# A shorter exponential on VectorE: one of three tensor products taken out of each group, by reading the score's bits as fp16

## The chip, the cores and the metric

One core of one Trainium2 chip. The metric is device time in microseconds (us), the median of several runs. All runs quoted here are fast ones; one run of the kernel before, at 1364.4 us, was slow and is left out everywhere.

## The reference

A transformer block with pre-normalisation: softmax attention with 32 heads of 16, then a GELU-gated feed-forward part.

```
B, S, D, H = 1, 2048, 512, 32           # Dh = 16, F = 1792
scores = einsum("bhqd,bhkd->bhqk", q, k) * Dh ** -0.5
p = softmax(scores, axis=-1)
o = einsum("bhqk,bhkd->bhqd", p, v)
h  = x + o.reshape(B, S, D) @ wo
h2 = h + (gelu(ln(h) @ w_gate) * (ln(h) @ w_up)) @ w_down
```

## The kernel before

The scores are 2048 tiles of 128x512 in PSUM. Most are exponentiated by ScalarE, two or three tiles an instruction (`exps`). Some are given to VectorE, which has no exponential: it converts the scaled score to a 16-bit integer whose upper bits are the power of two and whose lower ten bits are the fraction (`dconv`), and makes the exponential from those bits with a chain of 16-bit operations over a *group* of up to four tiles (`dchain`). The result has two terms: E, the bare power of two, and T, E times an odd cubic of the mantissa. TensorE multiplies both with V and lets PSUM add them.

```
def dconv(G, j, b):                     # one tile, PSUM to SBUF
    Op("dve", 0.7, tensor_scalar(out=dX[...], in0=pbank[:, b, :],
       scalar1=1024.0 * CENTER, scalar2=0.0, op0=add, op1=max))
# ... (cut)
def dchain(G):                          # one group of n tiles
    t1, t2 = 0.16 + 0.133 * n, 0.16 + 0.267 * n
    yield Wait(lambda: G["conv"] == n)
    Op("dve", t1, E = (X >> 3) & 0x1f80)              # power of two, as bf16 bits
    Op("dve", t1, X = (X & 0x3ff) | 0x3c00)           # mantissa M, as fp16 bits
    Op("dve", t2, W = M * M)
    Op("dve", t1, W = W * EK + EB)
    Op("dve", t2, W = W * M)
    C["gw"] += 1
    Op("dve", t2, T = W * E)                          # written over X
    G["done"] = 1
```

The order of all instructions is not written by hand. It is planned while the kernel is built: every `Op` states an assumed duration (the number behind the engine's name), and a list scheduler places the operations one after another in that assumed time. On the chip each engine then works through its list in that order (checked for VectorE: its 600 conversions and chain instructions come exactly as planned). A tile goes to VectorE when the plan sees VectorE free, a PSUM bank free, and the group before it far enough. Three constants of the plan are `LAT` (assumed delay between dependent operations), `SLACK` (a further delay for some), and `LOOK` (how much later an operation of an older stream may start and still be preferred).

```
lim = st + LOOK                         # st: earliest possible start on this engine
for r, s in cands:                      # by priority, then by age
    if r <= lim: ...                    # this one is taken
LAT = 0.12; SLACK = 0.3; LOOK = 0.12
```

The GELU of the feed-forward part runs between the attention work: VectorE copies the gate from PSUM to SBUF, GpSimd makes three operations on it, ScalarE a tanh, VectorE the rest. A guard at the end checks that all softmax sums lie in a range; if not, a second, slower path does everything again.

Of the kernel before, what the change touches and what calls it, by code (L numbers as in the profile page):

```python
# [163 lines left out]
BF16 = mybir.dt.bfloat16  # L164
ACT = mybir.ActivationFunctionType
ALU = mybir.AluOpType
# [886 lines left out]
F16, U16 = mybir.dt.float16, mybir.dt.uint16  # L1053
GS = 4
NX = 3
# [4 lines left out]
DGAP = 6.0  # L1060
DBUSY = 2.0
LN2 = 0.6931471805599453
CENTER = 40
EC, EB, EK = 0.45805388, 1.01669147, 0.16656247
VSCALE = 2.0 ** (127 - CENTER)


def bass_sequential_preLN__mha_block__geglu_ffn__prompt_kernel(nc, A_x, A_wqkv, A_wo, B_x, B_w_gate, B_w_up, B_w_down, out):
# [37 lines left out]
def fast_path(nc, P, base0, ARENA, pbank, flag, A_x, A_wqkv, A_wo, B_x, B_w_gate, B_w_up, B_w_down, out):  # L1106
# [3 lines left out]
    def at(name, shape, dt, off=None):  # L1110
        nb = DTS[dt]
        for d_ in shape[1:]:
            nb *= d_
        if off is None:
            off = cur[0]
            cur[0] = (off + nb + 31) // 32 * 32
        assert off + nb <= ARENA, ("SBUF arena overflow", name, off, nb, ARENA)
        return nc.alloc_sbuf_tensor_at(name, shape, dt, offset=base0 + off)
# [5 lines left out]
    PT = at("PT", [128, NRING, 512], BF16)  # L1124
    offX = cur[0]
    dX = at("dX", [128, NX, GS, 512], U16)
# [3 lines left out]
    probe = at("probe", [128, 2], U16)  # L1130
# [35 lines left out]
    ident32 = at("ident32", [128, 128], FP32)  # L1166
# [13 lines left out]
    LINV = at("LINV", [128, NUNIT, 16], FP32)  # L1180
    LCHK = at("LCHK", [128, NUNIT * 16 + 1], FP32, offPT)
# [10 lines left out]
    NU = len(units)  # L1192
# [27 lines left out]
    def ACTF(o, i, func, **kw):  # L1220
        return lambda e: e.activation(out=o, in_=i, func=func, **kw)  # L1221
# [23 lines left out]
    def consts():  # L1245
        yield Op("pool", 0.5, lambda e: e.memset(ones_bf[:], 1.0), writes=["ones_bf"])
        yield Op("pool", 0.3, lambda e: e.affine_select(out=ident[:], in_=ones_bf[:, 0:128], pattern=[[1, 128]], compare_op=ALU.is_equal, fill=0.0,
                                                        base=0, channel_multiplier=-1), reads=["ones_bf"], writes=["ident"])
        yield Op("pool", 0.1, lambda e: e.memset(nhalf[:], -0.5), writes=["nhalf"])
        yield Op("pool", 0.2, lambda e: e.memset(LINV[:], 1.0), writes=[("LINV", u) for u in range(NU)])  # L1250
        yield Op("pool", 0.1, lambda e: e.memset(zero_bf[:], 0.0), writes=["zero_bf"])
        yield Op("pool", 0.3, lambda e: e.tensor_copy(out=ident32[:], in_=ident[:]), reads=["ident"], writes=["ident32"])
        yield Op("pool", 2.3, lambda e: e.memset(VA[:, :, :, 16:17], VSCALE), writes=["VA_ones"])

    def masks():
        for par in range(2):
            iv = ident32[:].rearrange("p (g x i) -> p g x i", g=4, x=2)[:, :, par, :]
            yield Op("dve", 0.2, lambda e, iv=iv, par=par: e.tensor_reduce(out=qmask[:, par:par + 1], in_=iv, axis=AX.XY, op=ALU.add), reads=["ident32"], writes=[("qm", par)])
            yield Op("dve", 0.1, lambda e, par=par: e.tensor_scalar(out=qmask[:, par:par + 1], in0=qmask[:, par:par + 1], scalar1=256.0 / LN2, scalar2=None, op0=ALU.mult),
                     reads=[("qm", par)], writes=[("qm", par)])  # L1260
        yield Op("dve", 0.5, lambda e: e.memset(pbank[:, PVB, :], 0.0), writes=[("pb", PVB)])
        yield Op("dve", 0.1, lambda e: e.tensor_scalar(out=probe[:, 0:1], in0=ident32[:, 0:1], scalar1=1e6, scalar2=0.0, op0=ALU.add, op1=ALU.max), reads=["ident32"], writes=["probe"])


    def ln1(c):
# [97 lines left out]
    def proj_v():  # L1363
        for t in range(NT):
# [3 lines left out]
            for hf in range(2):  # L1368
                yield Op("pe", 2 * TMM, cols=1024, fns=[MM(pbank[:, b, :], xnT[:, dc, 128 * t:128 * t + 128], wqkv_sb[:, dc, 2 * D:3 * D], dc == 0, dc == 3)
                                      for dc in (2 * hf, 2 * hf + 1)], reads=rd, writes=[("pb", b)])  # L1370
            op = Op("dve", 0.61, lambda e, b=b, t=t: e.tensor_scalar(out=VA[:, t, :, 0:16], in0=pbank[:, b, :].rearrange("p (h i) -> p h i", i=16), scalar1=VSCALE, scalar2=None, op0=ALU.mult),
                    reads=[("pb", b)], writes=[("V", t)])
# [23 lines left out]
    def qk():  # L1396
        nxt, an = 0, 0
        while nxt < len(TILES):
# [57 lines left out]
            for i, j, db in late:  # L1456
                sch.add(dconv(G, j, db), -2)
# [22 lines left out]
    def exps():  # L1480
        st = 0
        while "qkdone" not in C or st < len(STEPS):
            if st >= len(STEPS):
                yield Wait(lambda: st < len(STEPS))
            an, mine, b0 = STEPS[st]
            p0, n = an % NRING, len(mine)
            yield Op("act", 0.093 + 0.427 * n, ACTF(PT[:, p0:p0 + n, :], pbank[:, b0:b0 + n, :], ACT.Exp, scale=LN2 / 1024, bias=-LN2 * (127 - CENTER) - math.log(EC)),
                     reads=[("pb", b0 + k) for k in range(n)], writes=[("PT", p0 + k) for k in range(n)],
                     gate=lambda: C.get("qk", 0) >= st + 1 and C["acons"] >= an + n - NRING)
            st += 1  # L1490
            C["exp"] = st
            made.update(mine)
        C["expdone"] = 1
        sch.early = True
        for b0, n in SLOTS:
            for b in range(b0, b0 + n):
                sch.release(b)
# [26 lines left out]
                C["dbanks"].append(b)  # L1524

    def dconv(G, j, b):
        yield Op("dve", 0.7, lambda e: e.tensor_scalar(out=dX[:, G["k"] % NX, j, :], in0=pbank[:, b, :], scalar1=1024.0 * CENTER, scalar2=0.0, op0=ALU.add, op1=ALU.max),  # L1527
                 reads=[("pb", b)], writes=[("dX", G["k"] % NX, j)], gate=lambda: C["gpv"] >= G["k"] - NX + 1)
        sch.release(b)
        G["conv"] += 1  # L1530

    def dchain(G):

        d, x, n = G["k"] % NE, G["k"] % NX, len(G["t"])
        X, W, E = dX[:, x, 0:n, :], dW[:, 0:n, :], dE2[:, d, 0:n, :]
        M, T = X.bitcast(F16), X.bitcast(BF16)
        kX, kW, kE = [("dX", x, j) for j in range(n)], ["dW"], [("dE", d)]
        t1, t2 = 0.16 + 0.133 * n, 0.16 + 0.267 * n
        yield Wait(lambda: G["conv"] == n)
        yield Op("dve", t1, lambda e: e.tensor_scalar(out=E.bitcast(U16), in0=X, scalar1=3, scalar2=0x1f80, op0=ALU.logical_shift_right, op1=ALU.bitwise_and), reads=kX, writes=kE,  # L1540
                 gate=lambda: C["gpv"] >= G["k"] - NE + 1)
        yield Op("dve", t1, lambda e: e.tensor_scalar(out=X, in0=X, scalar1=0x3ff, scalar2=0x3c00, op0=ALU.bitwise_and, op1=ALU.bitwise_or), reads=kX, writes=kX)  # L1542
        yield Op("dve", t2, lambda e: e.tensor_tensor(out=W, in0=M, in1=M, op=ALU.mult), reads=kX, writes=kW)  # L1543
        yield Op("dve", t1, lambda e: e.tensor_scalar(out=W, in0=W, scalar1=EK, scalar2=EB, op0=ALU.mult, op1=ALU.add), reads=kW, writes=kW)
        yield Op("dve", t2, lambda e: e.tensor_tensor(out=W, in0=W, in1=M, op=ALU.mult), reads=kW + kX, writes=kW)  # L1545
        C["gw"] += 1
        yield Op("dve", t2, lambda e: e.tensor_tensor(out=T, in0=W, in1=E, op=ALU.mult), reads=kW + kE, writes=kX)  # L1547
        G["done"] = 1

    def pv():  # L1550
# [230 lines left out]
    def check():  # L1781
        yield Wait(lambda: C.get(("hnT", NC - 1), 0) == CHUNKS[-1] // 128)
        lf = LINV[:].rearrange("p u i -> p (u i)")
        n = NUNIT * 16
        yield Op("dve", 0.1, lambda e: e.tensor_scalar(out=LCHK[:, n:n + 1], in0=probe[:, 0:1], scalar1=65535.0, scalar2=None, op0=ALU.is_equal), reads=["probe"] + [("LINV", u) for u in range(NU)], writes=["probe", "LCHK"])
        yield Op("dve", 0.4, lambda e: e.tensor_scalar(out=LCHK[:, 0:n], in0=lf, scalar1=2.0 ** -22, scalar2=2.0 ** 16, op0=ALU.max, op1=ALU.min),
                 reads=[("LINV", u) for u in range(NU)], writes=["LCHK"])
        yield Op("dve", 0.6, lambda e: e.tensor_tensor(out=LCHK[:, 0:n], in0=LCHK[:, 0:n], in1=lf, op=ALU.is_equal), reads=["LCHK"], writes=["LCHK"])
        yield Op("dve", 0.6, lambda e: e.tensor_reduce(out=lmin[:, 0:1], in_=LCHK[:], axis=AX.X, op=ALU.min), reads=["LCHK", "probe"], writes=["lmin"])
        b = yield Acquire(reads=["lmin", "ones_bf"])  # L1790
        yield Op("pe", 0.1, lambda e: e.matmul(pbank[0:1, b, 0:1], lmin[:, 0:1], ones_bf[:, 0:1], start=True, stop=True), reads=["lmin", "ones_bf"], writes=[("pb", b)])
        yield Op("dve", 0.1, lambda e: e.tensor_copy(out=flag[0:1, 0:1], in_=pbank[0:1, b, 0:1]), reads=[("pb", b)], writes=["flag"])
        P.flag_count = P.eng["dve"].count
        sch.release(b)
# [88 lines left out]
```

## Time and profile before

| | before |
|---|---|
| time, median | 948.25 us (4 runs, 947.93 to 949.04) |
| score tiles on ScalarE / VectorE | 1832 / 216 (in 64 groups) |
| busy: ScalarE, VectorE, GpSimd | 874.4, 735.3, 220.5 us of 947.0 |
| last exponential ends at | 912 us; what follows ("the tail"): 35 us |

From the page of the kernel before, the busy times by engine and the engines' shares of the chain that ended last (the path of work and waits, followed back from the last instruction):

```profile
PE 833.2 (88%) x7100; PEld 276.3 (29%) x7224; DVE 735.3 (78%) x1138; ACT 874.4 (92%) x817; POOL 220.5 (23%) x268
...
ACT 33%; PE 32%; DVE 16%; issue 14%; POOL 5%; ACTq 0%; DVEq 0%; POOLq 0%
```

ScalarE (ACT) is the busiest, and the chain passes mostly through it and TensorE (PE); 16% of it lies on VectorE (DVE).

Groups of instructions of the kernel before (count, busy us, mean ns of one, idle time of the engine before them and its releaser). A mean mixes shapes where it says "forms":

```profile
L1221 ACT ACTIVATE PT<-pbank 128x1536 bf16<-128x1536 f32 (+1 forms) x733 | 841.0, 1306 | 24.8 <-PE pbank L1215 24.2
L1527 DVE TENSOR_SCALAR dX<-pbank 128x512 uint16<-128x512 f32 x216 | 146.8, 686 | 45.9 <-PE pbank L1215 45.0
L1719 POOL TENSOR_TENSOR w_sb<-w_sb,g_sb 128x512 f32<-128x512 f32 (+1 forms) x56 | 71.3, 1273 | 4.7
L1717 POOL TENSOR_TENSOR w_sb<-g_sb 128x512 f32<-128x512 f32 (+1 forms) x56 | 65.3, 1166 | 168.2 <-DVE g_sb L1715 168.2
L1547 DVE TENSOR_TENSOR dX<-dW,dE_56 128x2048 bf16<-128x2048 f16 (+3 forms) x64 | 73.2, 1144 | 1.0
L1545 DVE TENSOR_TENSOR dW<-dW,dX 128x2048 f16<-128x2048 f16 (+3 forms) x64 | 71.0, 1109 | 1.4
L1543 DVE TENSOR_TENSOR dW<-dX 128x2048 f16<-128x2048 f16 (+3 forms) x64 | 70.7, 1105 | 1.2
L1726 ACT ACTIVATE w_sb<-w_sb 128x512 f32<-128x512 f32 (+1 forms) x56 | 34.1, 609 | 12.4 <-POOL w_sb L1719 12.4
```

The first line is the exponentials, the second the conversions (one for each VectorE tile), the POOL (GpSimd) lines two of the GELU steps, the three products below them the ones of the chain (L1545 is the one that goes), the last line the tanh of GELU. ScalarE waited 24.8 us in all before exponentials and 12.4 us before tanh, the latter for GpSimd.

Busy time by engine in two 40 us stretches, one with attention only and one that also carries feed-forward work (columns: stretch, its length, then each engine's busy us and instructions, granted TensorE clock, DMA share and GB/s):

```profile
core 0: us, PE busy (x) PEld busy (x) DVE busy (x) ACT busy (x) POOL busy (x), PEclk, DMA share, GB/s
160.00:200.00 40.00, 34.49 (x272) 10.04 (x275) 36.56 (x48) 39.40 (x36) 0.00 (x0) 1.00 0.03 8
320.00:360.00 40.00, 35.91 (x242) 11.14 (x247) 29.22 (x41) 38.85 (x40) 21.58 (x19) 1.00 0.00 1
```

In the first, ScalarE and VectorE are both nearly full. In the second GpSimd works for half of the time.

### The profile page before, as it was taken

What the parts mean: (1) busy time and instruction counts of PE and PEld (TensorE: products, weight loads), DVE (VectorE), ACT (ScalarE), POOL (GpSimd) and SP (SyncE); (2) the same over time, 40 slices, a digit from 0 to 9 for tenths busy, and PEclk for the clock granted to TensorE, in tenths of its full rate; (3) what the DMA queues carried; (4) which work ended last, traced back from release to release, by engine and by line L of the source; (5) the groups of instructions that cost most, each with busy time, mean ns of one, the idle gap of its engine ahead of it and who ended that gap; (6) DMA issues with size and microseconds to landing.
All of it is one profiled execution on the core that took longest, in us unless ns stands there. A gap on an engine that the chain in (4) does not pass through costs nothing.

```text
span 947.0 us, 17699 instructions
## 1 busy us (share of the span) xinstructions
PE 833.2 (88%) x7100; PEld 276.3 (29%) x7224; DVE 735.3 (78%) x1138; ACT 874.4 (92%) x817; POOL 220.5 (23%) x268
## 2 busy tenths in 40 slices
PE   8999888888898889888888988998898788899887
PEld 3322222222232222222222222222233222333345
DVE  7558989998979768699979788889958687643753
ACT  5789999999999999999999998999999799999962
POOL 6400000000027570000014564000003354302440
PEclk9999999999999999999999999999999899999999
DMA  5000006000000000000000000000000000000000
GB/s 178 1 1 1 1 1 244 1 2 1 12 2 1 1 1 12 23 1 2 1 12 1 1 1 1 12 23 1 1 8 19 1 1 1 2 12 24 2 7 21
DMA packets 12331, 15.13 MB, mean 16 GB/s; under 512 B 1744, under 2 KB 11216, under 8 KB 12240
## 3 DMA queue, kind: packets, MB, share of 16 engines
q1 hardware_dynamic: 12240, 13.90, 4.5%
q8 instruction: 59, 0.97, 0.5%
q14 instruction: 32, 0.26, 0.1%
HBM read 11.80 MB, written 2.10 MB: 15 GB/s over the span
## 4 chain that ended last, share of the span: by engine, by line
ACT 33%; PE 32%; DVE 16%; issue 14%; POOL 5%; ACTq 0%; DVEq 0%; POOLq 0%
ACT PT L1221 32%; PE pbank L1215 15%; PE pbank L1214 11%; PE pbank L1801 4%; POOL w_sb L1717 2%; DVE dX L1527 2%; POOL w_sb L1719 2%; DVE dW L1543 2%; DVE dE_56 L1540 1%; DVE dX L1542 1%; DVE dX L1547 1%; DVE g_sb L1715 1%; ACT w_sb L1726 1%; POOL w_sb L1718 1%; DVE w_sb L1727 1%
## 5 line engine op out<-in xcount | busy, mean ns | idle before, releaser
L1221 ACT ACTIVATE PT<-pbank 128x1536 bf16<-128x1536 f32 (+1 forms) x733 | 841.0, 1306 | 24.8 <-PE pbank L1215 24.2
L1215 PE MATMUL pbank<-QT,KT 32*128 32x512 bf16 (+1 forms) x2560 | 287.1, 341 | 71.7 <-ACT PT L1221 57.5
L1215 PE MATMUL pbank<-PT,VA 128*17 128x512 bf16 (+1 forms) x2307 | 187.6, 340 | 3.2 <-issue 1.8
L1527 DVE TENSOR_SCALAR dX<-pbank 128x512 uint16<-128x512 f32 x216 | 146.8, 686 | 45.9 <-PE pbank L1215 45.0
L1215 PEld LDWEIGHTS pbank<-QT,KT 32*128 32x128 bf16 x2560 | 77.0, 91 | 319.3 <-ACT PT L1221 220.6
L1801 PE MATMUL pbank<-ones_bf,zero_bf 128*128 128x512 bf16 x388 | 135.2, 388 | 13.5 <-DVE OA L1613 11.0
L1678 POOL TENSOR_SCALAR rstd_102<-mv_101 128x1 f32<-128x1 f32 x16 | 4.3, 269 | 510.4 <-DVE mv_101 L1676 510.3
L1717 POOL TENSOR_TENSOR w_sb<-g_sb 128x512 f32<-128x512 f32 (+1 forms) x56 | 65.3, 1166 | 168.2 <-DVE g_sb L1715 168.2
L1215 PEld LDWEIGHTS pbank<-PT,VA 128*17 128x17 bf16 x2307 | 47.5, 87 | 110.6 <-issue 98.1
L1547 DVE TENSOR_TENSOR dX<-dW,dE_56 128x2048 bf16<-128x2048 f16 (+3 forms) x64 | 73.2, 1144 | 1.0
L1719 POOL TENSOR_TENSOR w_sb<-w_sb,g_sb 128x512 f32<-128x512 f32 (+1 forms) x56 | 71.3, 1273 | 4.7
L1545 DVE TENSOR_TENSOR dW<-dW,dX 128x2048 f16<-128x2048 f16 (+3 forms) x64 | 71.0, 1109 | 1.4
L1543 DVE TENSOR_TENSOR dW<-dX 128x2048 f16<-128x2048 f16 (+3 forms) x64 | 70.7, 1105 | 1.2
L1801 PEld LDWEIGHTS pbank<-ones_bf,zero_bf 128*128 128x128 bf16 x459 | 37.3, 97 | 78.3 <-issue 61.7
L1727 DVE SCALAR_TENSOR_TENSOR w_sb<-w_sb,g_sb 128x512 f32<-128x512 f32 (+1 forms) x56 | 44.1, 787 | 20.6 <-ACT w_sb L1726 20.2
L1214 PE MATMUL pbank<-wd_sb,GUT 128*128 128x512 bf16 x211 | 56.0, 381 | 1.5 <-issue 1.3
L1715 DVE COPY g_sb<-pbank 128x512 f32<-128x512 f32 (+1 forms) x56 | 34.7, 619 | 18.6 <-PE pbank L1214 18.5
L1753 DVE SCALAR_TENSOR_TENSOR GUT<-pbank,w_sb 128x512 bf16<-128x512 f32 (+1 forms) x56 | 34.6, 619 | 15.5 <-PE pbank L1214 15.2
L1726 ACT ACTIVATE w_sb<-w_sb 128x512 f32<-128x512 f32 (+1 forms) x56 | 34.1, 609 | 12.4 <-POOL w_sb L1719 12.4
L1718 POOL TENSOR_SCALAR w_sb<-w_sb 128x512 f32<-128x512 f32 (+1 forms) x56 | 43.6, 779 | 4.9
L1540 DVE TENSOR_SCALAR dE_56<-dX 128x2048 uint16<-128x2048 uint16 (+3 forms) x64 | 43.5, 680 | 0.6
L1542 DVE TENSOR_SCALAR dX<-dX 128x2048 uint16<-128x2048 uint16 (+3 forms) x64 | 42.9, 670 | 1.2
(126 smaller groups left out, 694.0 us busy)
## 6 DMA issues: line engine op xcount, KB each, us to landing
xres<-in_A_x_dram SPq DMA_DIRECT2D x16, 128.0 KB, 2.2
out_dram<-out_sb SPq DMA_DIRECT2D x16, 128.0 KB, 1.7
wg_sb<-in_B_w_gate_dram SPq DMA_DIRECT2D x1, 1792.0 KB, 7.1
wu_sb<-in_B_w_up_dram SPq DMA_DIRECT2D x1, 1792.0 KB, 11.2
wd_sb<-in_B_w_down_dram SPq DMA_DIRECT2D x1, 1792.0 KB, 17.0
x_sb<-in_A_x_dram SPq DMA_DIRECT2D x3, 512.0 KB, 8.3
wqkv_sb<-in_A_wqkv_dram SPq DMA_DIRECT2D x1, 896.0 KB, 7.5
x_sb<-in_A_x_dram SPq DMA_DIRECT2D x2, 256.0 KB, 2.9
```

The lines of the kernel that those rows point to most:

```text
L1214: return lambda e: e.matmul(o, l, r, start=start, stop=stop)
L1215: return lambda e: e.matmul(o, l, r, start=start, stop=stop, tile_position=tile)
L1221: return lambda e: e.activation(out=o, in_=i, func=func, **kw)
L1527: yield Op("dve", 0.7, lambda e: e.tensor_scalar(out=dX[:, G["k"] % NX, j, :], in0=pbank[:, b, :], scalar1=1024.0 * CENTER, scalar2=0.0, o ...
L1543: yield Op("dve", t2, lambda e: e.tensor_tensor(out=W, in0=M, in1=M, op=ALU.mult), reads=kX, writes=kW)
L1545: yield Op("dve", t2, lambda e: e.tensor_tensor(out=W, in0=W, in1=M, op=ALU.mult), reads=kW + kX, writes=kW)
L1547: yield Op("dve", t2, lambda e: e.tensor_tensor(out=T, in0=W, in1=E, op=ALU.mult), reads=kW + kE, writes=kX)
L1717: yield Op("pool", 0.1 + 1.03 * nq / 512, lambda e: e.tensor_tensor(out=ws, in0=gs, in1=gs, op=ALU.mult), reads=[("g", i)], writes=[("w", i)])
L1718: yield Op("pool", 0.1 + 0.7 * nq / 512, lambda e: e.tensor_scalar(out=ws, in0=ws, scalar1=GA, scalar2=1.0, op0=ALU.mult, op1=ALU.add), re ...
L1719: yield Op("pool", 0.1 + 1.2 * nq / 512, lambda e: e.tensor_tensor(out=ws, in0=ws, in1=gs, op=ALU.mult), reads=[("w", i), ("g", i)], write ...
L1727: yield Op("dve", 0.1 + 0.7 * nq / 512, lambda e: e.scalar_tensor_tensor(out=ws, in0=ws, scalar=1.0, in1=gs, op0=ALU.add, op1=ALU.mult), r ...
L1801: fill_op = Op("pe", TMM, lambda e: e.matmul(pbank[:, PVB, :], zero_bf[:], ones_bf[:], start=False, stop=False, skip_group_check=True), re ...
```

## The change

The intent is to drop the product `W * M`. The score is now converted with 32768 added, so that its bits, read as fp16, are themselves minus the mantissa times the power of two: the factor that the last product needs. The polynomial has two terms (1 and EK times the square), a sign and a scale, and is written as bf16. So `T = (-EK*m*m - 1) * X_as_fp16`: two products instead of three. Constants, guard limits and the scale of V move along.

```diff
-CENTER = 40
-EC, EB, EK = 0.45805388, 1.01669147, 0.16656247
-VSCALE = 2.0 ** (127 - CENTER)
+XMIN = 32768.0
+CENTER = 12
+EC, EK = 0.46167356, 0.16665046
+ESCALE = 2.0 ** -80
+VSCALE = 2.0 ** (95 - CENTER)
 ... (bias of ScalarE's exponential, guard limits: cut)
-  dconv: scalar1=1024.0 * CENTER, scalar2=0.0
+  dconv: scalar1=XMIN + 1024.0 * CENTER, scalar2=XMIN
 ... (dchain, operands shortened)
-  t1  E = (X >> 3) & 0x1f80
-  t1  X = (X & 0x3ff) | 0x3c00
-  t2  W = M * M
-  t1  W = W * EK + EB
-  t2  W = W * M
-  t2  T = W * E
+  t1  W = (X & 0x3ff) | 0x3c00
+  t2  W = W * W
+  t1  WB = W * (-EK * ESCALE) - ESCALE          # bf16, over W
+  t1  E = (X >> 3) & 0x1f80
+  t2  T = WB * X.bitcast(F16)                    # written over X
```

Because the plan is made from the assumed durations, a shorter chain changes the order of everything, and which tiles go to VectorE.

More of the change, by code (lines that the diff above doesn't have):

```diff
@@ L1249, in consts @@
         yield Op("pool", 0.1, lambda e: e.memset(nhalf[:], -0.5), writes=["nhalf"])
-        yield Op("pool", 0.2, lambda e: e.memset(LINV[:], 1.0), writes=[("LINV", u) for u in range(NU)])
+        yield Op("pool", 0.2, lambda e: e.memset(LINV[:], 2.0 ** -10), writes=[("LINV", u) for u in range(NU)])
         yield Op("pool", 0.1, lambda e: e.memset(zero_bf[:], 0.0), writes=["zero_bf"])
@@ L1261, in masks @@
         yield Op("dve", 0.5, lambda e: e.memset(pbank[:, PVB, :], 0.0), writes=[("pb", PVB)])
-        yield Op("dve", 0.1, lambda e: e.tensor_scalar(out=probe[:, 0:1], in0=ident32[:, 0:1], scalar1=1e6, scalar2=0.0, op0=ALU.add, op1=ALU.max), reads=["ident32"], writes=["probe"])
+        yield Op("dve", 0.1, lambda e: e.tensor_scalar(out=probe[:, 0:1], in0=ident32[:, 0:1], scalar1=1e6, scalar2=XMIN, op0=ALU.add, op1=ALU.max), reads=["ident32"], writes=["probe"])
     def ln1(c):
@@ L1486, in exps @@
             p0, n = an % NRING, len(mine)
-            yield Op("act", 0.093 + 0.427 * n, ACTF(PT[:, p0:p0 + n, :], pbank[:, b0:b0 + n, :], ACT.Exp, scale=LN2 / 1024, bias=-LN2 * (127 - CENTER) - math.log(EC)),
+            yield Op("act", 0.093 + 0.427 * n, ACTF(PT[:, p0:p0 + n, :], pbank[:, b0:b0 + n, :], ACT.Exp, scale=LN2 / 1024, bias=-LN2 * (95 - CENTER) - math.log(EC)),
                      reads=[("pb", b0 + k) for k in range(n)], writes=[("PT", p0 + k) for k in range(n)],
@@ L1526, in dconv @@
     def dconv(G, j, b):
-        yield Op("dve", 0.7, lambda e: e.tensor_scalar(out=dX[:, G["k"] % NX, j, :], in0=pbank[:, b, :], scalar1=1024.0 * CENTER, scalar2=0.0, op0=ALU.add, op1=ALU.max),
+        yield Op("dve", 0.7, lambda e: e.tensor_scalar(out=dX[:, G["k"] % NX, j, :], in0=pbank[:, b, :], scalar1=XMIN + 1024.0 * CENTER, scalar2=XMIN, op0=ALU.add, op1=ALU.max),
                  reads=[("pb", b)], writes=[("dX", G["k"] % NX, j)], gate=lambda: C["gpv"] >= G["k"] - NX + 1)
@@ L1535, in dchain @@
         X, W, E = dX[:, x, 0:n, :], dW[:, 0:n, :], dE2[:, d, 0:n, :]
-        M, T = X.bitcast(F16), X.bitcast(BF16)
+        WB = W.bitcast(BF16)
         kX, kW, kE = [("dX", x, j) for j in range(n)], ["dW"], [("dE", d)]
@@ L1539, in dchain @@
         yield Wait(lambda: G["conv"] == n)
+        yield Op("dve", t1, lambda e: e.tensor_scalar(out=W.bitcast(U16), in0=X, scalar1=0x3ff, scalar2=0x3c00, op0=ALU.bitwise_and, op1=ALU.bitwise_or), reads=kX, writes=kW)
+        yield Op("dve", t2, lambda e: e.tensor_tensor(out=W, in0=W, in1=W, op=ALU.mult), reads=kW, writes=kW)
+        yield Op("dve", t1, lambda e: e.tensor_scalar(out=WB, in0=W, scalar1=-EK * ESCALE, scalar2=-ESCALE, op0=ALU.mult, op1=ALU.add), reads=kW, writes=kW)
         yield Op("dve", t1, lambda e: e.tensor_scalar(out=E.bitcast(U16), in0=X, scalar1=3, scalar2=0x1f80, op0=ALU.logical_shift_right, op1=ALU.bitwise_and), reads=kX, writes=kE,
                  gate=lambda: C["gpv"] >= G["k"] - NE + 1)
-        yield Op("dve", t1, lambda e: e.tensor_scalar(out=X, in0=X, scalar1=0x3ff, scalar2=0x3c00, op0=ALU.bitwise_and, op1=ALU.bitwise_or), reads=kX, writes=kX)
-        yield Op("dve", t2, lambda e: e.tensor_tensor(out=W, in0=M, in1=M, op=ALU.mult), reads=kX, writes=kW)
-        yield Op("dve", t1, lambda e: e.tensor_scalar(out=W, in0=W, scalar1=EK, scalar2=EB, op0=ALU.mult, op1=ALU.add), reads=kW, writes=kW)
-        yield Op("dve", t2, lambda e: e.tensor_tensor(out=W, in0=W, in1=M, op=ALU.mult), reads=kW + kX, writes=kW)
         C["gw"] += 1
-        yield Op("dve", t2, lambda e: e.tensor_tensor(out=T, in0=W, in1=E, op=ALU.mult), reads=kW + kE, writes=kX)
+        yield Op("dve", t2, lambda e: e.tensor_tensor(out=X.bitcast(BF16), in0=WB, in1=X.bitcast(F16), op=ALU.mult), reads=kW + kX, writes=kX)
         G["done"] = 1
@@ L1785, in check @@
         yield Op("dve", 0.1, lambda e: e.tensor_scalar(out=LCHK[:, n:n + 1], in0=probe[:, 0:1], scalar1=65535.0, scalar2=None, op0=ALU.is_equal), reads=["probe"] + [("LINV", u) for u in range(NU)], writes=["probe", "LCHK"])
-        yield Op("dve", 0.4, lambda e: e.tensor_scalar(out=LCHK[:, 0:n], in0=lf, scalar1=2.0 ** -22, scalar2=2.0 ** 16, op0=ALU.max, op1=ALU.min),
+        yield Op("dve", 0.4, lambda e: e.tensor_scalar(out=LCHK[:, 0:n], in0=lf, scalar1=2.0 ** -40, scalar2=2.0 ** -10, op0=ALU.max, op1=ALU.min),
                  reads=[("LINV", u) for u in range(NU)], writes=["LCHK"])
```

## The prediction

> **What bounds the kernel now.** ScalarE: 874.4 of 947.0 us (92%, engine table), of which 841.0 us are 733 exponentials (groups of instructions) over 1832 of the 2048 score tiles, 0.459 us a tile. VectorE makes the other 216 tiles, in 64 groups of one to four. By 40 us stretches ScalarE is at 38 to 40 of 40 from 80 to 680 us, except where the feed-forward part runs too (280-360, 520-600: 36 to 38); there the chain of waits passes through GpSimd, VectorE and TensorE. The last 37 us have no exponentials and stay. TensorE has room: 135.2 of its 833.2 busy us are filler products.
>
> **What the change removes.** One of three tensor-by-tensor products in each VectorE group. A group of four costs 4 conversions (0.686 each), shift 0.729, mask 0.738, product 1.242, polynomial 0.708, product 1.248, product 1.303 us. The middle product goes: 64 instructions, 71.0 us, about 1.25 us in a group of four (about 8.1 us start to start before, 6.9 after). The rest only changes buffers and 16-bit types. The Trainium skill ("VectorE: DVE Perf Modes", the perf-mode tier table) gives 16-bit tensor-by-tensor products 2x and scalar operations 4x; the traced product that already mixes fp16 with bf16 took 1303 against 1248 ns, so I expect no loss of mode. Work per tile on ScalarE and TensorE stays. The guard for the slow second path should stay quiet.
>
> **Where the gain goes.** VectorE is not the bound, so 71 us there is no 71 us of time. It pays only as far as the schedule, planned at build time from assumed durations, gives VectorE more tiles. In attention-only stretches (120-240, 360-480, 600-680) VectorE is mostly at 34 to 37 of 40 and a group starts every 8 to 9 us: it limits the tiles there, and a group 15% shorter should raise 126 tiles by about 22. Elsewhere (90 tiles) VectorE often waits for a score product or does GELU; I take 8 more. 30 tiles take 30 x 0.459 = 14 us off ScalarE and add 30 second value products and conversions where there is room. Some is lost in feed-forward stretches: 12 us off the span.
>
> Predicted time: **936 us** (-1.3%), range 924 to 945 (8 in 10); faster by over 2%: 0.20; within 2%: 0.77; slower by over 2%: 0.03.
>
> **What would show each step right or wrong.**
> - Five chain instructions a group instead of six, at unchanged durations for equal shapes (four tiles: products 1.24 to 1.31, scalar operations 0.7 us). A lost mode would show as twice that.
> - Conversions rise from 216 to 246 (235 to 260), groups to 70-78; exponentials fall to about 721, their busy time by 14 us.
> - VectorE's busy time falls by only 5 to 30 us: most freed time is filled again (about 1.95 us a tile).
> - The span falls by about as much as ScalarE's busy time, in the attention-only stretches; from 680 us on little changes.
>
> **What would make it wrong.** The plan opens no more groups (two PSUM banks, the least distance between groups, or waits for score products, 45.9 us already, limit it): then within 3 us. Or it opens many more, also in feed-forward stretches, because a shorter chain lets GELU work through sooner: 920 us or less. A re-planned order may put feed-forward work badly or well by chance, 5 us either way. If fp16 goes out of range and the guard fires, the time doubles.

## The result, and the profile after

The time is **936.32 us** (4 runs, 935.28 to 937.59), 0.9874 of before (95% interval 0.9856 to 0.9891). Ratios, here and below, are the mean time of one kernel's fast runs over that of the kernel before in the same rounds, so not quite the ratio of the medians. The predicted 936 us was met; the way there was not.

From the page of the kernel after, the same two lines:

```profile
PE 830.4 (89%) x7105; PEld 274.9 (29%) x7228; DVE 692.1 (74%) x1114; ACT 867.3 (93%) x811; POOL 210.3 (22%) x268
...
ACT 40%; PE 30%; issue 17%; DVE 8%; POOL 3%; DMA 1%; SPq 0%; ACTq 0%; DVEq 0%
```

VectorE's busy time fell by 43 us, not by 5 to 30, and its share of the chain halved (16% to 8%). GpSimd's busy time fell by 10 us with the same 268 instructions, which nothing in the diff touches.

The groups that answer to those shown before:

```profile
L1223 ACT ACTIVATE PT<-pbank 128x1536 bf16<-128x1536 f32 x727 | 833.8, 1300 | 20.7 <-PE pbank L1217 20.1
L1529 DVE TENSOR_SCALAR dX<-pbank 128x512 uint16<-128x512 f32 x231 | 156.8, 686 | 49.9 <-PE pbank L1217 47.8
L1720 POOL TENSOR_TENSOR w_sb<-g_sb 128x512 f32<-128x512 f32 (+1 forms) x56 | 60.0, 1072 | 168.6 <-DVE g_sb L1718 168.4
L1550 DVE TENSOR_TENSOR dX<-dW,dX 128x2048 bf16<-128x2048 bf16 (+3 forms) x69 | 77.4, 1122 | 1.2
L1545 DVE TENSOR_TENSOR dW<-dW 128x2048 f16<-128x2048 f16 (+3 forms) x69 | 75.5, 1094 | 1.4
L1722 POOL TENSOR_TENSOR w_sb<-w_sb,g_sb 128x512 f32<-128x512 f32 (+1 forms) x56 | 67.3, 1202 | 4.6
...
L1729 ACT ACTIVATE w_sb<-w_sb 128x512 f32<-128x512 f32 (+1 forms) x56 | 34.4, 614 | 9.8 <-POOL w_sb L1722 9.8
```

Conversions went from 216 to 231, not to 246; the exponentials' busy time fell by 7.2 us, not by 14. No operation lost its mode: for groups of four the last product took 1299 ns (1303 before) and the polynomial, now fp16 to bf16, 718 ns (708). That agrees with the Trainium skill ("VectorE: DVE Perf Modes", the perf-mode tier table), which gives for bf16 2x for products and 4x for scalar operations, about 1.22 and 0.69 us for 2048 elements; here, with fp16 and bf16, products that ran beside no GpSimd instruction took 1.22 us and scalar operations 0.69.

The same two stretches of the kernel after:

```profile
core 0: us, PE busy (x) PEld busy (x) DVE busy (x) ACT busy (x) POOL busy (x), PEclk, DMA share, GB/s
160.00:200.00 40.00, 33.90 (x282) 9.68 (x285) 36.26 (x51) 39.36 (x35) 0.00 (x0) 1.00 0.00 1
320.00:360.00 40.00, 36.53 (x256) 10.50 (x257) 32.55 (x45) 39.69 (x39) 20.06 (x19) 1.00 0.01 1
```

In the attention-only stretch VectorE was refilled, as predicted: over the stretches that the prediction named (120-240, 360-480, 600-680 us) conversions rose from 124 to 141, counted by where they start. Everywhere else they fell from 92 to 90, where I had counted on 8 more. (The prediction's 126 counts twice the two conversions that straddle an edge, and its 90 is the rest.)

Read along ScalarE, the 12.3 us of span split exactly, up to the last exponential and after it (taken from the trace):

| | before | after | difference |
|---|---|---|---|
| ScalarE busy up to the last exponential's end | 866.0 | 857.3 | -8.7 |
| ScalarE idle up to there | 46.0 | 34.2 | -11.8 |
| tail: from there to the end | 35.0 | 43.2 | +8.2 |
| span | 947.0 | 934.7 | -12.3 |

So the exponentials ended 20.5 us earlier, more than half of it from idle time that vanished, and the tail gave 8 us back. My prediction had no idle time in it and took the tail as fixed. The experiments ask where both come from.

### The profile page after: what moved, and what is told of

The parts are those of the page before. It is cut to its first block, busy times and chain, and to the rows that moved or that the text cites. A ratio compares the mean times of both kernels' runs of the same rounds, so it can differ in the third digit from the quotient of the medians.

```text
span 934.7 us, 17691 instructions
## 1 busy us (share of the span) xinstructions
PE 830.4 (89%) x7105; PEld 274.9 (29%) x7228; DVE 692.1 (74%) x1114; ACT 867.3 (93%) x811; POOL 210.3 (22%) x268
## 4 chain that ended last, share of the span: by engine, by line
ACT 40%; PE 30%; issue 17%; DVE 8%; POOL 3%; DMA 1%; SPq 0%; ACTq 0%; DVEq 0%
ACT PT L1223 38%; PE pbank L1217 15%; PE pbank L1216 11%; PE pbank L1804 3%; DVE g_sb L1718 1%; POOL w_sb L1722 1%; ACT w_sb L1729 1%; POOL w_sb L1720 1%; DVE dX L1529 1%; POOL w_sb L1721 1%; DMA wqkv_sb<-in_A_wqkv_dram 1%; DVE dX L1550 1%; DVE w_sb L1730 1%; PE pbank L1220 1%; DVE GUT L1756 1%
## 5 line engine op out<-in xcount | busy, mean ns | idle before, releaser
L1223 ACT ACTIVATE PT<-pbank 128x1536 bf16<-128x1536 f32 x727 | 833.8, 1300 | 20.7 <-PE pbank L1217 20.1
L1529 DVE TENSOR_SCALAR dX<-pbank 128x512 uint16<-128x512 f32 x231 | 156.8, 686 | 49.9 <-PE pbank L1217 47.8
L1720 POOL TENSOR_TENSOR w_sb<-g_sb 128x512 f32<-128x512 f32 (+1 forms) x56 | 60.0, 1072 | 168.6 <-DVE g_sb L1718 168.4
L1550 DVE TENSOR_TENSOR dX<-dW,dX 128x2048 bf16<-128x2048 bf16 (+3 forms) x69 | 77.4, 1122 | 1.2
L1545 DVE TENSOR_TENSOR dW<-dW 128x2048 f16<-128x2048 f16 (+3 forms) x69 | 75.5, 1094 | 1.4
L1216 PE MATMUL pbank<-hnT_c,wu_sb 128*128 128x512 bf16 (+1 forms) x271 | 64.5, 338 | 2.2 <-issue 1.3
L1216 PE MATMUL pbank<-hnT_c,wg_sb 128*128 128x512 bf16 (+1 forms) x267 | 62.4, 337 | 4.3 <-DVE GUT L1756 2.1
L1756 DVE SCALAR_TENSOR_TENSOR GUT<-pbank,w_sb 128x512 bf16<-128x512 f32 (+1 forms) x56 | 34.4, 617 | 16.6 <-PE pbank L1216 16.2
L1547 DVE TENSOR_SCALAR dE<-dX 128x2048 uint16<-128x2048 uint16 (+3 forms) x69 | 46.3, 671 | 0.0
L1546 DVE TENSOR_SCALAR dW<-dW 128x2048 bf16<-128x2048 f16 (+3 forms) x69 | 45.4, 658 | 0.6
L1544 DVE TENSOR_SCALAR dW<-dX 128x2048 uint16<-128x2048 uint16 (+3 forms) x69 | 44.9, 650 | 1.3
```

The costliest lines, as they stand in the source:

```text
L1216: return lambda e: e.matmul(o, l, r, start=start, stop=stop)
L1223: return lambda e: e.activation(out=o, in_=i, func=func, **kw)
L1529: yield Op("dve", 0.7, lambda e: e.tensor_scalar(out=dX[:, G["k"] % NX, j, :], in0=pbank[:, b, :], scalar1=XMIN + 1024.0 * CENTER, scalar2 ...
L1545: yield Op("dve", t2, lambda e: e.tensor_tensor(out=W, in0=W, in1=W, op=ALU.mult), reads=kW, writes=kW)
L1546: yield Op("dve", t1, lambda e: e.tensor_scalar(out=WB, in0=W, scalar1=-EK * ESCALE, scalar2=-ESCALE, op0=ALU.mult, op1=ALU.add), reads=kW ...
L1547: yield Op("dve", t1, lambda e: e.tensor_scalar(out=E.bitcast(U16), in0=X, scalar1=3, scalar2=0x1f80, op0=ALU.logical_shift_right, op1=ALU ...
```

## The experiments

Three theories stood at first. **1, tiles** (my prediction): the gain is the work that the plan moved off ScalarE. **2, waits**: the shorter chain itself lets the work behind it come earlier, with the order as it was. **3, chance**: a re-planned order is better or worse by as much as this.

### e1: the old order with the short chain

The planner still reserves the time of the third product, and emits nothing for it. Comparing the two plans operation by operation, all 4631 places are the same.

```diff
+  t1  E = (X >> 3) & 0x1f80                      # first, as in the kernel before
   t1  W = (X & 0x3ff) | 0x3c00
   t2  W = W * W
   t1  WB = W * (-EK * ESCALE) - ESCALE
-  t1  E = ...
+  t2  None                                       # planned, not emitted
   t2  T = WB * X.bitcast(F16)
```

> The order of all instructions and the 216 VectorE tiles of the kernel before, with the middle product taken out (216 conversions, 733 exponentials, VectorE busy down by about 70 us). Theory 1, the plan's extra tiles are the gain: at most 3 us faster than before (945 to 948 us). Theory 2, the shorter chain itself shortens waits of TensorE and ScalarE: most of the 12 us, 936 to 941 us. Theory 3, chance of re-planning: 947 to 948 us, as the order is not re-planned.

Measured: 939.55 us, 0.9906 of before (0.9885 to 0.9927). Its busy times, and its groups for the exponentials, two GELU steps and the tanh:

```profile
PE 829.9 (89%) x7100; PEld 276.0 (29%) x7224; DVE 668.6 (71%) x1074; ACT 873.6 (93%) x817; POOL 212.3 (23%) x268
```

```profile
L1228 ACT ACTIVATE PT<-pbank 128x1536 bf16<-128x1536 f32 (+1 forms) x733 | 841.0, 1307 | 21.7 <-PE pbank L1222 21.0
L1728 POOL TENSOR_TENSOR w_sb<-w_sb,g_sb 128x512 f32<-128x512 f32 (+1 forms) x56 | 67.6, 1207 | 4.7
L1726 POOL TENSOR_TENSOR w_sb<-g_sb 128x512 f32<-128x512 f32 (+1 forms) x56 | 64.1, 1146 | 165.1 <-DVE g_sb L1724 165.0
L1735 ACT ACTIVATE w_sb<-w_sb 128x512 f32<-128x512 f32 (+1 forms) x56 | 34.3, 613 | 5.8 <-POOL w_sb L1728 5.8
```

ScalarE does the same 841.0 us of exponentials, so not one tile was moved, and still about 9 us are gone (0.0094 x 948). For this gain theory 1 has fallen, and theory 3 too, as the order is frozen. What shrank is ScalarE's waiting: before exponentials from 24.8 to 21.7 us, before tanh from 12.4 to 5.8.

### e2: the new order with the long chain

The converse: the plan of the kernel after, with a third product emitted in each group for which the plan has no time. It writes E before E is made, so the result is unchanged; VectorE never stood idle before it (0.0 us in the trace), so the early write cost no wait of its own.

```diff
   t1   W = (X & 0x3ff) | 0x3c00
+  0.0  E = X.bitcast(F16) * X.bitcast(F16)
   t2   W = W * W
```

> The order and the 231 VectorE tiles of the kernel after, with a third product of the same size put back into every group (it writes a buffer that is overwritten later; result unchanged), in the plan at no time. VectorE busy about 765 us. Theory 1: VectorE has room for it, so 936 to 941 us. Theory 2: the waits come back, 946 us or more. Theory 3: as theory 1, 936 to 938 us.

Measured: 980.82 us, 1.0317 of before (1.0288 to 1.0347), some 42 us above the kernel after (0.0317 + 0.0126, times 948).

```profile
L1223 ACT ACTIVATE PT<-pbank 128x1536 bf16<-128x1536 f32 x727 | 837.7, 1284 | 57.3 <-PE pbank L1217 56.0
```

VectorE was busy for 58.8 us more than in the kernel after (750.9 against 692.1) and had, by its busy share of 74%, ample room. Yet ScalarE's waiting for scores went from 20.7 to 57.3 us. The mean granted TensorE clock fell from 0.992 to 0.968: the trace has 14 stretches at half clock, against 4 after. The Trainium skill ("TensorE: Matmul & The Clock Gate", What's actually happening) says that the clock falls to half after an idle window of about 3.4 us, and these stretches do last 3.41 us or two or three times that, the last one of the trace apart. But the windows were not idle: in the 3.41 us before the other 13, TensorE was busy for 30 to 55%, and its longest idle stretch there was 2.04 us. Here the measurement decides: shorter gaps were enough. Of the 40.7 us that ScalarE idled longer than in the kernel after, 23.0 lie within half-clock stretches and 17.7 outside, so the half-clock stretches do not hold all of it; beyond that, clock and lateness were not separated, and the lower clock may itself follow from the lateness. TensorE's waits for conversions and chain results (dX) rose from 4.0 to 20.3 us. The run speaks for theory 2 against 1: VectorE's time is not spare, whatever its busy share.

### e5: the same VectorE time without the product

Why does ScalarE wait less in e1? Rivals: (A) VectorE's *time*, since what stands behind the product in its order comes sooner; (B) the *kind* of operation. The Trainium skill ("SBUF — State Buffer", Who interferes with whom) says that a VectorE instruction with two SBUF inputs contends with a GpSimd instruction that reads SBUF, that whichever comes first holds the shared ports for its whole length, and that a `tensor_reduce` on trn2 never contends. GELU's three middle steps are on GpSimd, so a product can delay GELU. This trace agrees. In the kernel before, at one place, VectorE, GpSimd and ScalarE:

```profile
728.05 1.22 DVE L1545 TENSOR_TENSOR dW<-dW,dX 128x2048 f16<-128x2048 f16 x1
...
730.12 2.06 DVE L1547 TENSOR_TENSOR dX<-dW,dE_56 128x2048 bf16<-128x2048 f16 x1
```

```profile
728.22 1.52 POOL L1718 TENSOR_SCALAR w_sb<-w_sb 128x512 f32<-128x512 f32 x1
729.83 1.27 POOL L1719 TENSOR_TENSOR w_sb<-w_sb,g_sb 128x512 f32<-128x512 f32 x1
731.06 2.02 POOL L1717 TENSOR_TENSOR w_sb<-g_sb 128x512 f32<-128x512 f32 x1
```

```profile
735.27 0.63 ACT L1726 ACTIVATE w_sb<-w_sb 128x512 f32<-128x512 f32 x1 [0.58 <-POOL w_sb L1719]
...
739.13 0.63 ACT L1726 ACTIVATE w_sb<-w_sb 128x512 f32<-128x512 f32 x1 [0.98 <-POOL w_sb L1719]
...
743.06 1.45 ACT L1221 ACTIVATE PT<-pbank 128x1536 bf16<-128x1536 f32 x1 [2.39 <-PE pbank L1215]
```

(Start, duration, then the instruction, and in brackets the engine's idle time before it and what ended it.) The product at 728.05 starts first and keeps its 1.22 us; the GpSimd step that starts during it (728.22) takes 1.52 instead of the 0.62 that it takes at best. The product at 730.12 starts while GpSimd is still at work and takes 2.06, and GpSimd's square, which starts during that product, takes 2.02 instead of the 1.04 that it takes when undisturbed. The tanh instructions that follow keep ScalarE waiting.

So e5 is e1 with a reduction put where the product had been, as long as the product (42 of them on groups of four, 1252 ns in the mean), but with one SBUF input.

```diff
-  t2  None                                       # e1: planned, not emitted
+  t2  lmin[:, 4:5] = max over dX[:, x, 0:n, 0:264]   # never read
```

> The first experiment (old order, 216 tiles, short chain) with a VectorE reduction in the place of the missing product: as long as the product (about 1.25 us in a group of four), but with one SBUF input. Theory A, what counts is VectorE's time, as work behind it in its order comes late: back to 945 to 950 us. Theory B, what counts is that a product with two SBUF inputs keeps GpSimd from SBUF and so slows GELU: stays at 938 to 942 us, and GpSimd busy stays at about 212 us instead of 220.

Measured: 942.83 us, 0.9940 of before (0.9920 to 0.9960).

```profile
PE 853.1 (91%) x7224; PEld 276.5 (29%) x7224; DVE 732.1 (78%) x1138; ACT 874.1 (93%) x817; POOL 210.9 (22%) x268
```

```profile
L1554 DVE TENSOR_REDUCE lmin<-dX 128x1 bf16<-128x1056 f16 x42 | 52.6, 1252 | 1.0
L1228 ACT ACTIVATE PT<-pbank 128x1536 bf16<-128x1536 f32 (+1 forms) x733 | 841.3, 1303 | 24.5 <-PE pbank L1222 23.9
L1735 ACT ACTIVATE w_sb<-w_sb 128x512 f32<-128x512 f32 (+1 forms) x56 | 34.2, 610 | 5.3 <-POOL w_sb L1728 5.1
```

VectorE's busy time is back at 732 us, GpSimd's stays at 211, and the two waits go different ways: before tanh it stays low (5.3), so that part is the kind of operation; before exponentials it is back (24.5), so that part is VectorE's time. The reductions are as long as planned, and the eight four-tile ones that met a GpSimd instruction took 1.25 us like the rest (products that met one: 1.53 in the mean, before); the GpSimd step that started 0.17 us into the one at 724.26 took its undisturbed 0.62. In microseconds, about 5.7 of e1's 8.9 remain (0.0060 against 0.0094 of 948): roughly two thirds from contention with GpSimd, one third from VectorE's time. The time fell between the two forecasts. The two runs were on different chips and their intervals overlap: e5 lies 3.2 us above e1, uncertain by nearly as much (an estimate from the two intervals), so the split is rough. A reduction also writes almost nothing, which a product does not; that the page names the second input and not the write is an argument, not a measurement. Nor are products alone in this: in the kernel before, the four-tile shift, with one input, took 0.69 us with no GpSimd instruction beside it and 0.99 in the mean of the six that met one.

How VectorE's time reaches ScalarE shows in TensorE's waits for the last product of the chain (it makes T, which TensorE multiplies with V), in the kernel before, e1 and e5 (total us, times, longest):

```profile
PE pbank L1215 <- DVE dX L1547: 6.7, 7, 2.8
```

```profile
PE pbank L1222 <- DVE dX L1556: 2.6, 2, 2.0
```

```profile
PE pbank L1222 <- DVE dX L1556: 5.4, 7, 2.0
```

They fall by 4.1 us and come back by 2.8; ScalarE's waits for scores, which TensorE makes in the same list, fall by 3.1 and come back by 2.8.

### e6: a second product less, in the frozen new order

Is the relief used up? The square is planned and not emitted (a wrong result; relative error 0.027).

```diff
-  t2  W = W * W
+  t2  None
```

> The kernel after with its order frozen and the square taken out as well (wrong result on purpose in the VectorE tiles). Theory A with relief that goes on: 926 to 931 us, as much again as the first product gave. Theory A with relief that is used up (ScalarE and the end of the feed-forward part bind): 932 to 936 us. The tail after the last exponential stays above 40 us if the feed-forward part of the last chunk but one binds it.

Measured: 926.93 us, 0.9771 of before (0.9751 to 0.9790), about 10 us below the kernel after, with the same 727 exponentials. The second product less gives as much as the first, so the relief is not used up. The tail stayed long, 41.6 us: it goes with the order. The frozen new order had 43.2, 43.0 (e2) and 41.6 us, the frozen old one 35.0, 35.1 (e1) and 34.9 (e5).

Where the tail comes from can be read from ScalarE's timeline. Before:

```profile
910.04 1.99 ACT L1221 ACTIVATE PT<-pbank 128x1024 bf16<-128x1024 f32 x2
911.85 0.48 ACT L1726 ACTIVATE w_sb<-w_sb 128x256 f32<-128x256 f32 x1
...
923.82 1.26 ACT L1732 ACTIVATE w_sb<-pbank 128x256 f32<-128x256 f32 x3 [0.70 <-PE pbank L1214]
```

And after:

```profile
890.35 1.20 ACT L1223 ACTIVATE PT<-pbank 128x1024 bf16<-128x1024 f32 x1
...
901.10 0.42 ACT L1729 ACTIVATE w_sb<-w_sb 128x256 f32<-128x256 f32 x1 [2.40 <-POOL w_sb L1722]
...
911.58 1.26 ACT L1735 ACTIVATE w_sb<-pbank 128x256 f32<-128x256 f32 x3 [7.56 <-PE pbank L1216]
```

L1732 and L1735 are the last chunk's GELU. Before, one tanh of the chunk before it was left when the exponentials ended, and the last GELU began 12 us later. After, five were left, the last of them at 901.1 us, then 28 products with w_down, and the last GELU began 20 us after the last exponential. The order had put attention ahead of the feed-forward work of the fourth chunk, which then bound the end. A faster attention alone does not do this: over all runs but e8, the tail is 34.9 to 35.1 us with at most one tanh behind the last exponential in ScalarE's order, 35.7 to 36.3 with two or three and 39.0 to 43.2 with five; and e4 below, whose exponentials ended 4 us earlier still, left three.

### e3, e4, e7, e9, e10, e11: other plans of both kernels

One constant of the planner is changed by a few per cent. That says nothing about the work, and gives another order.

```diff
-SLACK = 0.3
+SLACK = 0.35            # e3 (before), e4 (after)
-LAT = 0.12
+LAT = 0.125             # e7 (before), e8 (after; see below), e9 (after, with LOOK = 0.125)
+LAT = 0.11              # e10 (after), e11 (before)
```

> The kernel before, with one constant of the planner changed (SLACK 0.3 to 0.35): still 216 VectorE tiles, other order. Theories 1 and 2: 945 to 951 us, chance is worth 3 us. Theory 3, chance is worth as much as the change: off by 6 us or more either way.

> The kernel after with the same constant changed: still 231 VectorE tiles, other order. Theories 1 and 2: 933 to 940 us. Theory 3: off by 6 us or more either way.

> The kernel before with another planner constant changed (LAT 0.12 to 0.125; 218 VectorE tiles). If chance of the plan is worth some 5 us: 942 to 953 us.

> The kernel after with LAT 0.12 to 0.125 as in the run that fell onto the second path, and LOOK raised with it (0.12 to 0.125), so that the planner may again prefer the older of two open groups whose next instruction is LAT away (231 tiles). If the interleaving of two groups over the one scratch buffer was what fired the guard: correct on the first path, 925 to 942 us. If it was the range of fp16: 2410 us again.

> The kernel after with LAT 0.12 to 0.11 (LOOK stays above it; 235 tiles). One more plan of the change: 925 to 940 us if plans scatter by some 5 us about 931.

> The kernel before with the same constant (217 tiles): 945 to 955 us, and its partner 10 to 22 us below it, if the change is worth that much on any plan.

| plan | before: us (VectorE tiles) | after: us (VectorE tiles) | difference |
|---|---|---|---|
| as given | 948.25 (216) | 936.32 (231) | -11.9 |
| SLACK 0.35 (e3, e4) | 949.37 (216) | 925.90 (231) | -23.5 |
| LAT 0.11 (e11, e10) | 953.65 (217) | 943.41 (235) | -10.2 |
| LAT 0.125 (e7, e9) | 954.09 (218) | 934.76 (231) | -19.3 |
| mean | 951.3 | 935.1 | -16.2 |

Theory 3 holds as a second term: with the work unchanged, the kernel before lies between 948 and 954 us and the kernel after between 926 and 943, so one plan is worth up to 17 us, more than the change as given. e4 has the same 231 tiles as the kernel after and is 10 us faster; e10 has four more and is 7 us slower. Tile counts within this range do not explain the times. The traces show what does, of e4 at least: its exponentials have 727 instructions like the kernel after and ScalarE's work is the same, but its tail is 6.9 us shorter (36.3 against 43.2) and ScalarE idles 4.0 us less before it. In all four pairs the change wins, by 10 to 24 us. The last pair differs in LOOK and in the chip as well, so it is a looser pair. e7 and e10 came out just above what I had expected of them.

Split as above, by the profiled runs, the four pairs lose 16.7 us of span in the mean: 7.8 of ScalarE's work (6 to 9 in each pair), 10.0 of its idle time up to the last exponential (1 to 16), while the tail grows by 1.2. So theory 1 was not empty: the tiles give 6 to 9 us in every pair, the waits about as much in the mean, and it is the waits and the tail that the plan scatters.

### e8: a plan on which the guard fired

> The kernel after with the same change (234 VectorE tiles). If the change itself is worth 10 to 20 us over any pair of plans: 925 to 938 us, and 8 us or more below its partner; if its gain was chance, within 5 us of its partner.

Measured: 2410.13 us, correct. The guard fired in all runs, and the second path did the work again. Two causes were open: a score out of the smaller range that fp16 leaves, or a wrong value made on the first path. VectorE's timeline of e8 where its order first goes wrong:

```profile
171.96 0.69 DVE L1547 TENSOR_SCALAR dE<-dX 128x2048 uint16<-128x2048 uint16 x1
172.56 0.69 DVE L1544 TENSOR_SCALAR dW<-dX 128x2048 uint16<-128x2048 uint16 x1
173.28 1.22 DVE L1550 TENSOR_TENSOR dX<-dW,dX 128x2048 bf16<-128x2048 bf16 x1
```

The mask of the *next* group (L1544, which writes the single scratch buffer W) stands between the shift and the last product of *this* group (L1550, which still reads W). The planner has no rule that forbids it. It only prefers the older group, and it can do that only if the older group's next operation, ready LAT after its last, falls within LOOK. With LAT 0.125 and LOOK 0.12 it does not. e9 tests this: the same LAT, LOOK raised to 0.125, and it ran on the first path (934.76 us, correct), with no such place in its trace, against nine in e8's. e7, the kernel before with LAT 0.125, interleaves groups as well (12 times) and stayed correct: there the first two instructions of a group touch E and X only. The change made W live from a group's first instruction, so the same slip now destroys it.

### e12: a version meant to beat both

Two tiles of the same row group are allowed in one group, so that groups fill sooner (243 tiles).

```diff
-  ... if i not in own and TILES[i][2] not in G["g"] | used]
+  ... if i not in own and TILES[i][2] not in used]
-LAT = 0.12
+LAT = 0.11
```

> A version to beat both: the partner of the change with LAT 0.11, and two tiles of the same row group allowed in one VectorE group (243 tiles instead of 235). 8 tiles fewer on ScalarE are 3.7 us, VectorE has 14 us more to do: 922 to 932 us, faster than its partner only by chance or by up to 4 us.

Measured: 944.83 us, against 943.41 of its partner e10. Eight more tiles took 1.9 us off the exponentials' busy time (833.9 to 832.0), and ScalarE's idle time before them rose from 30.2 to 33.8 us. No gain, where I had expected 922 to 932 us. The fastest correct kernel is e4, the change with SLACK 0.35: 925.90 us, 0.9762 of before.

## Why the prediction was right in time and wrong in its steps

- **Removed work: right.** Five instructions a group instead of six, durations and modes unchanged.
- **"VectorE is not the bound, so 71 us there is no 71 us of time": right in size, but the next sentence failed.** "It pays only as far as the schedule ... gives VectorE more tiles" is the step that the runs refuted. e1 moved no tile and gained about 9 us; e6 took away another product and gained 10 more. What stands in its place: every VectorE instruction stands in a fixed order in front of results that TensorE waits for and of GELU steps, and a product beside GpSimd also holds up GpSimd. Both end as waits of ScalarE.
- **30 more tiles and 14 us of exponentials: half.** 15 tiles and 7.2 us. In the attention-only stretches it was nearly right (17 of the 22 tiles); elsewhere I counted 8 more and there were 2 fewer. Conversions (231) and groups (69) fell just outside my ranges.
- **VectorE's busy time down by 5 to 30 us: wrong** (43 us), since fewer tiles came back.
- **"The last 37 us ... stay" and "from 680 us on little changes": wrong twice.** The last exponential ended 20.5 us earlier, of which some 8 us were won after 680 us (the kernel after had as many tiles done at 668 us as the one before at 680), and then the tail took 8.2 us back.
- **"A re-planned order may put feed-forward work badly or well by chance, 5 us either way": right in kind, too small.** Plans of the kernel after differ by up to 17 us.
- **The guard: it stayed quiet in the given kernel**, but fired for a reason that I had not thought of, a buffer that two groups share.

The terms, about -7 for tiles, -9 for waits with the order frozen, +8 for the tail and a rest of about -4, which is only what is left over, add to the -12 that I had predicted from one term. The agreement is luck: the tiles gave half of what I had counted on, and waits and tail, which I had not counted, happened to make up the difference. Not settled: how far contention and VectorE's time each carry beyond the rough split of e5, and which decision of the plan leaves e4 a shorter tail than the kernel after.

## What to carry to other kernels

When each engine executes a fixed order, the time of an engine that is not the busiest is not free: freeze the order and take the work out (and put it in) to see what it is worth, before counting the work that a new plan moves. When a small edit re-plans everything, measure several plans of both versions before crediting the edit, because one plan can be worth more than the change. And a scratch buffer shared by two streams needs a rule in the planner, not a tie-break that happens to hold.

## What the Trainium skill lacked or had wrong

- "Perfetto Trace Analysis", Identifying the Most-Contended Engine: it says to optimise the engine of highest occupancy first. Taken alone this would pass over VectorE, though the section after it (Optimization Strategy) goes on to the gaps of that engine and what they wait for, which is what paid here; it has no figure for such a case. Here ScalarE was at 92% and VectorE at 78%, and 67 us taken off VectorE in an unchanged order (e1) gave about 9 us without touching ScalarE's work; some 59 us of busy time put onto VectorE at 74% (e2) cost about 42 us.
- "SBUF — State Buffer", Who interferes with whom: right, but without a figure for elementwise work of both engines. Of the 126 four-tile products of the kernel before, the 108 with no GpSimd instruction beside them took 1.22 us; the 18 that met one took 1.53 us in the mean and up to 2.17. GpSimd's square of 128x512 took 1.04 us undisturbed and up to 2.02. Reductions of e5 took 1.25 us with and without one.
- No page has what a product beside GpSimd costs at the end of a chain over three engines: e1 and e5 lowered ScalarE's wait for the tanh input from 12.4 to 5.8 and 5.3 us.
- "TensorE: Matmul & The Clock Gate", What's actually happening: its 3.4 us window shows in the half-clock stretches of e2 (3.41 us and multiples), but not its condition, an idle window: TensorE was busy for 30 to 55% of the 3.41 us before them, with no idle stretch over 2.04 us. (The page tells elsewhere of a clock that swings with short idles, without such figures.)
